# The first steps of a fused attention and two-layer-network kernel, issued from a written list of named steps

## The chip, the cores and the metric

The kernel runs on one core of one Trainium2 chip. The metric is the device time of one execution in microseconds (us), and the number compared is the median of several executions. The engines are named as the profile names them: PE is TensorE (matmuls; PEld its weight loads), DVE is VectorE, ACT is ScalarE, POOL is GpSimd, and SP is the engine whose queue issues nearly all DMAs. Each engine runs its own instructions strictly in the order in which the program issued them. What an instruction needs from another engine it waits for, and everything behind it on its engine waits too.

## What is computed

Attention over pooled keys and values (8 batches, 8 heads, 576 rows, pooling by 8 to 72 keys), then two networks on the 4608 resulting rows of 512 numbers. This change touches only the beginning: the attention of the first rows and `h = x @ w_in` with the first steps behind it.

```python
k_p = k.reshape(B, H, Sp, pool, D).mean(axis=3)      # pool = 8, Sp = 72
v_p = v.reshape(B, H, Sp, pool, D).mean(axis=3)
scores = scale * np.matmul(q, k_p.transpose(0, 1, 3, 2))
scores = scores - np.max(scores, axis=-1, keepdims=True)
attn = np.exp(scores)
attn = attn / (np.sum(attn, axis=-1, keepdims=True) + 1e-09)
x = np.matmul(attn, v_p)            # then rows x 512
h = x @ w_in                        # 4608 x 512 @ 512 x 2048
g = h * np.cos(h)
y = g @ w_out                       # 2048 x 512; a second network follows
```

## The kernel before

**Tiling.** The 4608 rows are nine blocks of 512. A block's attention runs over four pairs of heads. Its result x is kept as a high and a low part, four pairs of them, one for each quarter of the 512 columns. The first matrix product is cut in units: a unit is one block times 256 columns of `w_in`, that is two chunks of 128 columns, and has eight slots of three matmuls each (line 652: high by high, high by low, low by high). Slots 0 to 3 of a unit use its first chunk with x quarters 0 to 3, slots 4 to 7 its second chunk. Counted over the whole kernel, slot 64 is the first slot of unit 8. The first sixteen units take blocks 0 and 1 in turn (`units_h`): units 0 to 4 are block 0 with chunks 0 to 9, units 5 to 9 block 1 with the same chunks, units 10 to 15 the other six chunks for both blocks.

**A chunk of weights** comes as 64-bit words and is turned into a high and a low float part by class `Chunk`: `load` (an SP DMA), `s1` (two ACT instructions, lines 114 and 115), `bits` (three DVE instructions, 119, 123 and 127), `join` (POOL, 139), then the high part by ACT (line 1173) and the low part by POOL (line 1174).

**The attention of a block**, for each pair: scores on PE (line 449 for block 0, 414 for block 1), maximum and subtraction on DVE (460 to 470, 422 and 423), exponentials on ACT (464, 480), sums on DVE and a scaling of the exponentials (`norm`, lines 499 to 514) on POOL or DVE, transposes on PE (550, 528), a high part by ACT and a low part by DVE for each, the product with the values on PE (577), and x in two parts by ACT (579) and DVE (580). The keys of block 1 are pooled by PE (line 250), the values of both by PE (304, 307) and prepared on DVE, ACT and POOL (`prep_vn`).

**Behind a unit** runs `chain`: step 0 on ACT (663), step 1 on DVE (666), step 2 on ACT (669, a sine) and step 3 on DVE (671), which frees the unit's PSUM tile. There are three such tiles, so a unit cannot start before step 3 of the unit three before it. `g_store` sends the result to DRAM.

**What sets the order.** Block 0's attention is written out as plain calls, with the chunks advanced by `pipe.step()` (class `Pipe`) in between; a step runs the word operations of one chunk, the high and low part of the one before, and the first step of the next. Then a loop goes over the units' slots. Behind each slot's matmuls it issues the chain steps at fixed slots, a `pipe.step()` at slot 1 and in the first units at slot 5, and what `Attn.plan` has put in the list `work` for that slot. Block 1's plan is spread over the first five units by the factor `Q0 / NQ` = 5/8, block 2's begins at slot 64. So issue order is fixed by the program, and each engine sees its own share of it.

Of the kernel before, what the change touches and what calls it, by code (L numbers as in the profile page):

```python
# [20 lines left out]
POOL = 8  # L21
TWO_PI = 2.0 * math.pi
# [13 lines left out]
def fused_kernel(ctx, tc, qT_d, kT_d, vN_d, vM_d, vL_d, w_in, w_out, w2_in, w2_out, g_ln, out):  # L36
# [64 lines left out]
    class Chunk:  # L101
# [39 lines left out]
        def s2(self):  # L141
            self.bits()
            self.join()

        def s3(self):
            self.done(self)

# [22 lines left out]
    class Pipe:  # L170


        def __init__(self, chunks):
            self.todo = list(chunks)
            self.loaded, self.one, self.two = [], [], []

        def fill(self, most=8):

            held = [c.raw for c in self.loaded + self.one]
            while self.todo and len(held) < most:  # L180
                c, raw = self.todo[0]
                if raw is not None and any(raw is r for r in held):
                    break
                self.todo.pop(0)
                c.load(raw)
                held.append(raw)
                self.loaded.append(c)

        def step(self):
            last = self.two.pop(0) if self.two else None  # L190
            if self.one:
                c = self.one.pop(0)
                c.s2()
                self.two.append(c)
            if last:
                last.s3()
            self.fill()
            if self.loaded:
                c = self.loaded.pop(0)
                c.s1()  # L200
                self.one.append(c)

        @property
        def busy(self):
            return self.loaded or self.one or self.two or self.todo


# [13 lines left out]
    def kv_jobs(b, hf):  # L221


        def raw_tile(n):
            if b < 2:
                return wi.tile([P, n], F32, "kvraw")
            return wo.tile([P, n], F32, "kvraw")
# [6 lines left out]
        def k_job(i):  # L234
            p = 2 * hf + i
            raw = raw_tile(POOL * SP)
# [27 lines left out]
        def v_job(i):  # L264
# [3 lines left out]
            raw = raw_tile(POOL * D)  # L268
# [13 lines left out]
    def load_vn(b):  # L282
        if b == 0:
            t = [wi.tile([P, 2, BLK], F32, "vn") for _ in range(3)]
# [95 lines left out]
    class Attn:  # L380
# [49 lines left out]
        def scores0(self, p):  # L430
            self.e[p] = self.tile([P, TPB, 2, SP], F32, "e")
            e, qT = self.e[p], self.qT[p]
            if p != 2:
                pool, tag = (ps_q, "q") if p == 3 else (ps_y, "y")
                sc = pool.tile([P, 2, BLK], F32, tag=tag, name="sc")
                parts = [(sc[:, :, 0:4 * SP].rearrange("p u (t m) -> p u t m", t=2), 0, TPB)]
            else:
                parts = [(None, 2 * u, 2) for u in range(TPB // 2)]
            direct = p % 2 == 0
            if direct:  # L440
                self.sm[p] = ap2.tile([P, 2 * TPB], F32, tag="sm", name="sm", bufs=4)
            for sc, t0, nt in parts:
                if sc is None:
                    sc = ps_a.tile([P, 2, 2 * SP], F32, tag="a", name="sc")
                    sc = sc.rearrange("p (u t) m -> p u t m", u=1)
# [7 lines left out]
                u = nt // 2  # L453
                mx = ap2.tile([P, 2 * TPB], F32, tag="mx0", name="mx")[:, 0:2 * nt]
                mxv = mx.rearrange("p (u g) -> p u g", u=u)
                sc = sc.rearrange("p u t (a s) -> p u (t a) s", a=2)
                ev = e[:, t0:t0 + nt].rearrange("p (u t) a s -> p u (t a) s", u=u)
                if direct:
                    sm = self.sm[p][:, 2 * t0:2 * (t0 + nt)]
                    nc.vector.tensor_reduce(out=mxv, in_=sc, axis=AX.X, op=ALU.max, negate=True)  # L460
                    nc.vector.tensor_scalar(
                        out=mx, in0=mx, scalar1=SCALE, scalar2=None, op0=ALU.mult)
                    for g in range(2 * nt):
                        nc.scalar.activation(
# [713 lines left out]
    def now(fns):  # L1178
        for fn in fns:
            fn()  # L1180
# [355 lines left out]
```

## Time and profile before

| | us |
|---|---|
| median of 3 runs | 1328.03 (1328.01 to 1330.66) |
| the profiled execution, its own time | 1331.27 |
| its span, first to last instruction | 1329.5 |
| PE busy in the span | 1302.5 |
| DVE busy | 1053.0 |
| ACT busy | 697.9 |
| POOL busy | 504.5 |

The page shows busy time of each engine and the span in 40 slices of 33 us, with the clock that was granted to TensorE. A view of stretches gives the busy time between chosen instants. The view of waits says which engine stood still and what ended the wait. The timeline lists instructions in order of time, with equal ones merged. A wait is put down to the instruction that ended last before it.

### The profile page before, as it was taken

To read this page: it belongs to the slowest core of one execution; us is meant where nothing else is said; L and a number is where in the kernel's file an instruction comes from. 1 tells how busy PE (TensorE), PEld (TensorE's weight loads), DVE (VectorE), ACT (ScalarE), POOL (GpSimd) and SP (SyncE) were. 2 spreads that over 40 slices of the span, in tenths; PEclk is the share of its full clock that TensorE was granted. 3 is DMA by queue.
4 is the path that set the end of the run, shared out by engine and by line. 5 is a ranking of instruction groups with operands and counts; after the bars stand their busy time and mean duration, and the time that the engine had idled before them with its cause. 6 is when DMAs were issued, how large, how long until landed. Compare 5 with 4: busy or idle time off the path is not lost. (4 is left out here: it accounts for less than half of the span.)

```text
span 1329.5 us, 20583 instructions
## 1 busy us (share of the span) xinstructions
PE 1302.5 (98%) x7574; PEld 1140.3 (86%) x7574; DVE 1053.0 (79%) x1675; ACT 697.9 (52%) x987; POOL 504.5 (38%) x668
## 2 busy tenths in 40 slices
PE   6889999999999999999999999999999999999998
PEld 5768888888888888899999999998778888888887
DVE  7798888989788775879989889985687777776754
ACT  4576757756566657544444444443444444444432
POOL 3487678776574425301101001102434434343410
PEclk9899999999999999999999999999999999999999
DMA  8415567785674627655555455568310111111101
GB/s 287 172 68 191 187 231 270 254 289 188 222 254 145 226 98 255 234 196 158 172 141 176 132 173 175 160 219 341 105 56 33 56 40 49 47 45 51 40 25 40
DMA packets 82133, 206.09 MB, mean 155 GB/s; under 512 B 7920, under 2 KB 26352, under 8 KB 82032
## 3 DMA queue, kind: packets, MB, share of 16 engines
q1 hardware_dynamic: 81888, 204.77, 45.7%
q8 instruction: 60, 0.98, 0.3%
q14 instruction: 41, 0.34, 0.1%
q10 hardware_dynamic: 144, 0.00, 0.0%
HBM read 125.57 MB, written 79.17 MB: 154 GB/s over the span
## 5 line engine op out<-in xcount | busy, mean ns | idle before, releaser
L652 PE MATMUL h<-x,w 128*128 128x512 f32 x1728 | 433.6, 400 | 0.0
L652 PEld LDWEIGHTS h<-x,w 128*128 128x128 f32 x1728 | 316.5, 189 | 62.7 <-issue 2.2
L744 PE MATMUL y<-g,wy 128*128 128x256 f32 x3024 | 363.8, 283 | 1.3 <-DVE g L718 0.7
L744 PEld LDWEIGHTS y<-g,wy 128*128 128x128 f32 x3024 | 363.2, 192 | 1.9 <-DVE g L718 1.1
L716 ACT CAST g<-gs 128x1024 fp32r<-128x1024 f32 x72 | 75.7, 1051 | 173.2 <-PE y L744 86.1
L139 POOL TENSOR_TENSOR dec<-dec,raw 128x512 int32<-128x512 int32 x24 | 33.6, 1401 | 241.4 <-DVE dec L127 227.4
L718 DVE TENSOR_TENSOR g<-gs,g 128x1024 fp32r<-128x1024 f32 x72 | 90.5, 1257 | 34.2 <-ACT g L716 32.2
L669 ACT ACTIVATE t<-t,cst 128x1024 f32<-128x1024 f32 x72 | 83.1, 1154 | 62.3 <-DVE t L666 62.1
L974 POOL TENSOR_TENSOR yl<-yr,yh 128x1024 fp32r<-128x1024 f32 x18 | 43.9, 2439 | 153.7 <-ACT yh L969 117.6
L663 ACT ACTIVATE t<-h 128x1024 int32<-128x1024 f32 x72 | 73.5, 1020 | 53.7 <-PE h L652 53.5
L671 DVE TENSOR_TENSOR t<-t,h 128x1024 f32<-128x1024 f32 x72 | 87.3, 1212 | 11.9 <-ACT t L669 11.9
L666 DVE SCALAR_TENSOR_TENSOR t<-t,h 128x1024 f32<-128x1024 int32 x72 | 87.2, 1212 | 1.5 <-ACT t L663 1.5
L231 POOL TENSOR_TENSOR kvraw<-kvraw 128x256 f32<-128x256 f32 (+1 forms) x124 | 83.0, 670 | 11.5 <-DMA kvraw<-in_vM 3.5
L1105 POOL TENSOR_TENSOR sc<-sc,cst 128x1 f32<-128x1 f32 x36 | 20.3, 565 | 141.3 <-DVE sc L1094 114.0
L1140 ACT COPY o<-o 128x512 f32<-128x512 f32 x36 | 21.1, 587 | 96.4 <-PE o L1158 96.4
L698 DVE TENSOR_TENSOR gs<-gr,gs 128x256 f32<-128x256 f32 x136 | 65.9, 484 | 4.7
L718 DVE TENSOR_TENSOR g<-gr,g 128x768 fp32r<-128x768 f32 x68 | 69.1, 1017 | 0.0
L1156 PE MATMUL o<-w,lh 128*128 128x512 f32 x176 | 69.1, 393 | 0.0
L1158 PE MATMUL o<-w,ll 128*128 128x512 f32 x176 | 68.6, 390 | 0.0
L1157 PE MATMUL o<-w,lh 128*128 128x512 f32 x176 | 68.6, 390 | 0.0
L716 ACT CAST g<-gr 128x768 fp32r<-128x768 f32 x68 | 56.6, 833 | 0.0
L139 POOL TENSOR_TENSOR wf<-dec,raw 128x512 int32<-128x512 int32 x24 | 31.9, 1331 | 64.4 <-ACT eL L532 46.4
(191 smaller groups left out, 2572.3 us busy)
## 6 DMA issues: line engine op xcount, KB each, us to landing
gd<-t SPq DMA_DIRECT2D x72, 512.0 KB, 3.1
gr<-gd SPq DMA_DIRECT2D x68, 512.0 KB, 4.0
raw<-in_w_in SPq DMA_DIRECT2D x24, 512.0 KB, 4.4
raw<-in_w_out SPq DMA_DIRECT2D x24, 512.0 KB, 4.4
kvraw<-in_kT SPq DMA_DIRECT2D x32, 288.0 KB, 4.5
qT<-in_qT SPq DMA_DIRECT2D x36, 256.0 KB, 4.8
yd<-yo SPq DMA_DIRECT2D x36, 256.0 KB, 4.4
yr<-yd SPq DMA_DIRECT2D x18, 512.0 KB, 4.0
```

What stands on the lines that cost most here:

```text
L231: nc.gpsimd.tensor_tensor(out=x[:, 0:m], in0=x[:, 0:m], in1=x[:, m:2 * m], op=ALU.add)
L652: nc.tensor.matmul(h_ps[n][:, i], lhsT=w[:, a, kk, :], rhs=x[:, b], start=(kk == 0 and m == 0), stop=(kk == KD - 1 and m == 2),)
L663: nc.scalar.activation(out=t.bitcast(I32), in_=h, func=AF.Copy, scale=1.0 / TWO_PI, bias=0.25)
L666: nc.vector.scalar_tensor_tensor(out=t, in0=t.bitcast(I32), scalar=-TWO_PI, in1=h, op0=ALU.mult, op1=ALU.add)
L669: nc.scalar.activation(out=t, in_=t, func=AF.Sin, bias=halfpi)
L671: nc.vector.tensor_tensor(out=t, in0=t, in1=h, op=ALU.mult)
L716: nc.scalar.copy(out=o, in_=f)
L718: nc.vector.tensor_tensor(out=o, in0=f, in1=flat(g[i - 1])[:, 0:n * NH].bitcast(F32), op=ALU.subtract)
L744: nc.tensor.matmul(y_ps[j][i][:, NH * c:NH * (c + 1)], lhsT=w[:, a, P * c:P * (c + 1)], rhs=g[y][b], start=(q == 0 and c == 0 and k == 0), ...
L1156: nc.tensor.matmul(ps, lhsT=hi, rhs=w[:, 0], start=(c == 0), stop=False)
L1157: nc.tensor.matmul(ps, lhsT=hi, rhs=w[:, 1], start=False, stop=False)
L1158: nc.tensor.matmul(ps, lhsT=lo, rhs=w[:, 0], start=False, stop=(c == NF2 - 1))
```

## The change

The calls of the beginning, `Pipe`, and the plan of block 1 are gone. In their place each piece of work is a named step in a table, and a string `ORDER` lists 390 steps. Those ahead of the first `|` are issued before the first unit. Each following group, between two `|`, is issued behind the matmuls of one slot, for the first sixteen units (128 slots). From unit 16 on the old rule holds. Blocks 2 and on keep their plan.

The names: `LK`, `LQ`, `LV` are loads of keys, queries, values; a digit pair is block and pair. `S` scores (a: PE, b: DVE, c: ACT exponentials), `X` the exponentials of block 1, `N` norm (a: sums; b on POOL, `B` on DVE), `T`, `E` transposes (a PE, b ACT, c DVE), `V`, `P` values, `A` the x of a pair (a PE, b ACT, c DVE). `C5l`, `C5a`, `C5b`, `C5j`, `C5h` are load, `s1`, `bits`, `join` and high part of chunk 5; `C5o` is its low part on POOL, `C5O` on DVE. `H5.1` is chain step 1 of unit 5, `G5` its store.

The steps do what they did, but for two things. The low parts of chunks 0, 1, 2, 3, 5, 9, 10, 13 and 15 are on DVE (all sixteen were on POOL). Of block 0's four scalings pair 0's is on DVE and pairs 1 to 3 are on POOL (pairs 1 and 3 were on DVE, 0 and 2 on POOL). The scores of block 0's pair 2 are two steps for its two halves. The order of the first loads changes as well, and `mx0` has four buffers in place of two. Which SBUF slot a block 0 or 1 tile takes follows from the order of issue.

```diff
+ORDER = """
+LK00 LQ00 LK01 LG LK02 LQ01 LQ02 LK03 C0l LQ03 LV0 LK11 C2l LV1 LK13 C4l C3l LQ11 C1l LK12 LK10
...
+C1j C1h A02b C2b K10 C1O C2j A03c K11 C3a S100a C3b C3j C2h C2O C6l K12 C4a | A02c |  |  |  |
...
-        def s2(self):
-            self.bits()
-            self.join()
...
-    class Pipe:
-        def step(self):
-            last = self.two.pop(0) if self.two else None
-            if self.one:
-                c = self.one.pop(0)
-                c.s2()
-                self.two.append(c)
-            if last:
-                last.s3()
-            self.fill()
-            if self.loaded:
-                c = self.loaded.pop(0)
-                c.s1()
-                self.one.append(c)
...
-            def scale():
-                for i, (p, e) in enumerate(zip(ps, es)):
-                    i2 = p % 2
-                    eng = nc.vector if self.j == 0 and i2 else nc.gpsimd
+            def scale(i, eng):
+                p, e = ps[i], es[i]
+                i2 = p % 2
...
-            nc.gpsimd.tensor_tensor(
-                out=t[:, 1], in0=c.f, in1=t[:, 0].bitcast(F32), op=ALU.subtract)
...
+        def lo(eng):
+            eng.tensor_tensor(
+                out=t[0][:, 1], in0=c.f, in1=t[0][:, 0].bitcast(F32), op=ALU.subtract)
...
+        steps.update({f"C{f}l": load, f"C{f}a": c.s1, f"C{f}b": c.bits, f"C{f}j": c.join,
+                      f"C{f}h": hi, f"C{f}o": lambda: lo(nc.gpsimd), f"C{f}O": lambda: lo(nc.vector)})
...
+        places = [line.split() for line in ORDER.strip().split("|")]
+        for name in places[0]:
+            steps[name]()
...
                 h_mm(n, s // KD, s % KD)
-                if n > 1 and s == 3:
-                    chain(n - 2, 3)
-                if n > 0 and s in (0, 4, 7):
-                    chain(n - 1, (0, 4, 7).index(s))
-                if n > 1 and s == 5:
-                    g_store(n - 2)
-                if s == 1 and pipe.busy or s == 5 and n < Q0 - 1:
-                    pipe.step()
+                if n < 2 * NQ:
+                    for name in places[1 + SL * n + s]:
+                        steps[name]()
+                else:
...
                 for fn in work[SL * n + s]:
                     fn()
```

How this moves instructions shows in the order in which each engine gets them. `raw_170` to `raw_173` are the word buffers of chunks 0 to 3, `raw` that of a later chunk; `kT_90` to `kT_93` are the key tables of batch 0, `kT_94` to `kT_97` those of batch 1.

DVE, block 0's first pairs, before: the sums of pair 0 stand behind the maximum and subtraction of pair 1, and the scaling of pair 0 is not here (POOL has it).

```order
L460 TENSOR_REDUCE mx<-sc 128x8
L461 TENSOR_SCALAR mx<-mx 128x8
L243 TENSOR_REDUCE kp<-kvraw 128x72
L245 COPY kT_92<-kp 64x72
L246 COPY kT_92<-kp 64x72
L469 TENSOR_REDUCE mx<-sc 128x8
L470 TENSOR_TENSOR e<-sc,mx 128x576
L502 TENSOR_SCALAR sm<-sm 128x8
L503 RECIPROCAL sm<-sm 128x8
```

The same place on DVE now.

```order
L439 TENSOR_REDUCE mx<-sc 128x8
L441 TENSOR_SCALAR mx<-mx 128x8
L220 TENSOR_REDUCE kp<-kvraw 128x72
L222 COPY kT_92<-kp 64x72
L223 COPY kT_92<-kp 64x72
L485 TENSOR_SCALAR sm<-sm 128x8
L486 RECIPROCAL sm<-sm 128x8
L491 TENSOR_TENSOR em<-e,sm 128x4x128
L496 TENSOR_TENSOR el<-e,sm 128x4x32 x2
L439 TENSOR_REDUCE mx<-sc 128x8
L444 TENSOR_TENSOR e<-sc,mx 128x576
```

The scaling of pair 0 has come to DVE, and pair 1's maximum and subtraction stand behind it.

DVE, the end of block 0's attention (line 580) and the first scores of block 1 (422, 423), before.

```order
L580 TENSOR_TENSOR x<-xo,x 128x512 x2
L119 TENSOR_SCALAR dec<-dec 128x512
L123 TENSOR_SCALAR dec<-dec 128x512
L127 SCALAR_TENSOR_TENSOR dec<-raw_172,dec 128x512
L119 TENSOR_SCALAR dec<-dec 128x512
L123 TENSOR_SCALAR dec<-dec 128x512
L127 SCALAR_TENSOR_TENSOR dec<-raw_173,dec 128x512
L119 TENSOR_SCALAR dec<-dec 128x512
L123 TENSOR_SCALAR dec<-dec 128x512
L127 SCALAR_TENSOR_TENSOR dec<-raw,dec 128x512
L422 TENSOR_REDUCE mx<-sc 128x4
L423 TENSOR_TENSOR e<-sc,mx 128x288
```

The same place now; line 1151 is a low part on DVE.

```order
L564 TENSOR_TENSOR x<-xo,x 128x512
L141 TENSOR_SCALAR dec<-dec 128x512
L145 TENSOR_SCALAR dec<-dec 128x512
L149 SCALAR_TENSOR_TENSOR dec<-raw_173,dec 128x512
L1151 TENSOR_TENSOR w<-dec,w 128x512
L564 TENSOR_TENSOR x<-xo,x 128x512
L141 TENSOR_SCALAR dec<-dec 128x512
L145 TENSOR_SCALAR dec<-dec 128x512
L149 SCALAR_TENSOR_TENSOR dec<-raw,dec 128x512
L399 TENSOR_REDUCE mx<-sc 128x4
L400 TENSOR_TENSOR e<-sc,mx 128x288
L1151 TENSOR_TENSOR w<-dec,w 128x512
```

The words of chunks 0 to 3 are now done before the last x of block 0, and one chunk's words, not three, stand between that x and the first scores of block 1.

PE, the first units, before.

```order
L652 MATMUL h<-x,w 128x512 x6
L414 MATMUL sc<-kT_90,qT 64x144
L414 MATMUL sc<-kT_94,qT 64x144
L414 MATMUL sc<-kT_94,qT 128x144
L652 MATMUL h<-x,w 128x512 x3
L250 MATMUL kp<-kvraw,ident 128x72 x8
L652 MATMUL h<-x,w 128x512 x3
L414 MATMUL sc<-kT_94,qT 128x144 x2
L652 MATMUL h<-x,w 128x512 x6
```

The same place on PE now.

```order
L227 MATMUL kp<-kvraw,ident 128x72 x16
L391 MATMUL sc<-kT_90,qT 64x144
L391 MATMUL sc<-kT_94,qT 64x144
L391 MATMUL sc<-kT_94,qT 128x144
L227 MATMUL kp<-kvraw,ident 128x72 x8
L628 MATMUL h<-x,w 128x512 x15
L391 MATMUL sc<-kT_94,qT 128x144 x2
L628 MATMUL h<-x,w 128x512 x3
L227 MATMUL kp<-kvraw,ident 128x72 x8
```

Three of the four key poolings and the first half of block 1's first scores now stand ahead of the first unit, and five slots of that unit run before the second half of the scores.

## Rows read from the trace of the kernel before

**Rows 1.** The page's 40 slices of the span: PE busy in tenths.

```profile
PE   6889999999999999999999999999999999999998
```

**Rows 2.** Stretches of the span: busy us (and instructions) of each engine, clock.

```profile
core 0: us, PE busy (x) PEld busy (x) DVE busy (x) ACT busy (x) POOL busy (x), PEclk, DMA share, GB/s
0.00:38.77 38.77, 26.51 (x122) 21.59 (x122) 28.91 (x72) 18.97 (x59) 15.65 (x36) 0.91 0.81 276
...
0.00:101.81 101.81, 81.54 (x389) 64.89 (x390) 83.94 (x154) 60.30 (x127) 59.26 (x83) 0.92 0.51 177
60.00:101.81 41.81, 37.90 (x189) 28.98 (x188) 40.39 (x64) 32.47 (x50) 33.02 (x39) 1.00 0.19 69
101.81:119.50 17.69, 17.69 (x79) 14.65 (x78) 16.24 (x16) 11.19 (x15) 13.88 (x15) 1.00 0.45 154
119.50:200.00 80.50, 80.50 (x410) 67.09 (x409) 66.38 (x101) 52.82 (x68) 55.65 (x83) 1.00 0.60 214
28.00:34.00 6.00, 5.06 (x15) 3.75 (x15) 5.67 (x12) 3.04 (x7) 2.19 (x2) 0.50 0.31 93
48.00:58.00 10.00, 9.21 (x34) 8.05 (x35) 4.95 (x9) 3.26 (x8) 5.21 (x4) 0.51 0.43 151
```

**Rows 3.** Waits of PE, 0 to 100 us: total, times, longest.

```profile
PE sc L449 <- DVE kT L246: 5.2, 1, 5.2
PE sc L414 <- DVE e L423: 4.1, 1, 4.1
PE eTp L550 <- DVE eT L555: 3.0, 2, 1.7
```

**Rows 4.** Timeline of PE: start, us, what; in brackets the idle before.

```profile
49.72 2.94 PE L652 MATMUL h<-x,w 128*128 128x512 f32 x6
...
99.77 19.90 PE L652 MATMUL h<-x,w 128*128 128x512 f32 x87
119.50 0.65 PE L414 MATMUL sc<-kT,qT 128*128 128x144 f32 x4
```

**Rows 5.** Waits of DVE, 0 to 102 us.

```profile
DVE mx L422 <- PE sc L414: 5.6, 2, 4.9
...
DVE eL L533 <- ACT eL L532: 2.2, 1, 2.2
```

**Rows 6.** Timeline of DVE and ACT up to 11 us.

```profile
0.84 0.65 DVE L1221 MEMSET kT<- 128x144 f32 x4 [0.84 <-PEq L1522]
...
7.55 0.76 DVE L460 TENSOR_REDUCE mx<-sc 128x8 f32<-128x576 f32 x1 [2.38 <-PE sc L449]
...
10.78 0.76 DVE L469 TENSOR_REDUCE mx<-sc 128x8 f32<-128x576 f32 x1 [0.61 <-PE sc L449]
10.90 0.24 ACT L464 ACTIVATION_READ_ACCUMULATOR e<-sc,mx 128x1 f32 x1
```

**Rows 7.** Timeline of all engines, 43 to 48 us: word steps beside POOL's work.

```profile
43.63 0.69 DVE L127 SCALAR_TENSOR_TENSOR dec<-raw,dec 128x512 int32<-128x512 int32 x1
...
44.24 0.42 DVE L119 TENSOR_SCALAR dec<-dec 128x512 f32<-128x512 f32 x1
44.56 1.28 POOL L139 TENSOR_TENSOR dec<-dec,raw 128x512 int32<-128x512 int32 x1 [1.24 <-DVE dec L127]
44.70 1.42 DVE L123 TENSOR_SCALAR dec<-dec 128x512 int32<-128x512 int32 x1
45.79 1.44 POOL L1174 TENSOR_TENSOR w<-dec,w 128x512 fp32r<-128x512 f32 x1
...
46.15 1.63 DVE L127 SCALAR_TENSOR_TENSOR dec<-raw,dec 128x512 int32<-128x512 int32 x1
```

**Rows 8.** Timeline of DVE: a scaling of block 0, and block 1's last x.

```profile
18.01 0.69 DVE L509 TENSOR_TENSOR em<-e,sm 128x512 f32<-128x512 f32 x1
18.62 0.49 DVE L514 TENSOR_TENSOR el<-e,sm 128x128 f32<-128x128 f32 x2
...
101.13 0.68 DVE L580 TENSOR_TENSOR x<-xo,x 128x512 fp32r<-128x512 f32 x1
```

More of the change, by code (lines that the diff above doesn't have):

```diff
@@ L283, in load_vn @@
         if b == 0:
-            t = [wi.tile([P, 2, BLK], F32, "vn") for _ in range(3)]
+            t = [wi.tile([P, 2, BLK], F32, "vn", i) for i in range(4, 7)]
         else:
@@ L435, in scores0, with mm @@
                 sc = pool.tile([P, 2, BLK], F32, tag=tag, name="sc")
[L436 to L438 removed]
+                sc = sc[:, :, 0:4 * SP].rearrange("p u (t m) -> p u t m", t=2)
+                t0, nt = 0, TPB
+            else:
+                sc = ps_a.tile([P, 2, 2 * SP], F32, tag="a", name="sc")
+                sc = sc.rearrange("p (u t) m -> p u t m", u=1)
+                t0, nt = 2 * u0, 2
             direct = p % 2 == 0
[L440 removed]
+            if direct and u0 == 0:
                 self.sm[p] = ap2.tile([P, 2 * TPB], F32, tag="sm", name="sm", bufs=4)
[L442 to L445, printed above, removed]
+            u = nt // 2
+            mx = ap2.tile([P, 2 * TPB], F32, tag="mx0", name="mx", bufs=4)[:, 0:2 * nt]
+            mxv = mx.rearrange("p (u g) -> p u g", u=u)
+            sv = sc.rearrange("p u t (a s) -> p u (t a) s", a=2)
+            ev = e[:, t0:t0 + nt].rearrange("p (u t) a s -> p u (t a) s", u=u)
+            def mm():
                 for i in range(nt):
@@ L474, in scores0, with exps @@
                     )
-            if not direct:
-                self.exp(p)
+            def exps():
+                if not direct:
+                    return self.exp(p)
+                sm = self.sm[p][:, 2 * t0:2 * (t0 + nt)]
+                for g in range(2 * nt):
+                    nc.scalar.activation(
+                        out=ev[:, g // 4, g % 4], in_=sv[:, g // 4, g % 4], func=AF.Exp,
+                        bias=mx[:, g:g + 1], scale=SCALE, accum_out=sm[:, g:g + 1],
+                    )
+            return mm, less, exps
         def exp(self, p):
@@ L581, in av @@
                     out=x[:, 1], in0=o, in1=x[:, 0].bitcast(F32), op=ALU.subtract))
-        def now(self, name, *a):
-            for fn in getattr(self, name)(*a):
-                fn()
         def plan(self, put):
@@ L637, in fused_kernel @@
     gd = [dram.tile([P, NQ, 2, BLK], F32, tag="gd", name=f"gd{j}") for j in range(NB)]
-    w_in_t, w_op = [], [{} for _ in range(NQ)]
+    w_in_t, w_op = {}, [{} for _ in range(NQ)]
+    steps = {}
     h_ps, h_t, g_raw, g_sum, g_t, y_ps = {}, {}, {}, {}, {}, {}
@@ L1270, in fused_kernel @@
-        now(prep_vn(0, 1))
-        a0.now("av", 1)
-        a0.now("e_tr", 3)
-        a0.now("e_tr_left", 1)
-        pipe.step()
-        a0.now("av", 2)
-        add(1, 0, "k0")
-        a0.now("av", 3)
-        add(1, 0, "k1")
-        pipe.step()
-        early = {7: raws[1], 9: raws[2], 11: raws[3]}
-        pipe.todo += [(order[i], early.get(i)) for i in range(6, len(order))]
-        pipe.step()
+            in_=m_key.rearrange("p (o s) -> p o s", o=1)[:, :, 0:KL].to_broadcast([P, 16, KL]))
```

279 lines of the change are left out of this document (137 added, 142 removed).

## The prediction

> **What bounds the kernel now.** I read the slices first [rows 1]. PE is at 9 tenths or more everywhere but in the first two slices, so only the beginning has anything to give. The stretches then put numbers on it [rows 2]: up to 101.81 us PE is busy for 81.54, so it idles 20.27 us, and behind that it has no gap (17.69 of 17.69 us, then 80.50 of 80.50). Part of the busy time is slow as well: in 28 to 34 and 48 to 58 us the granted clock is half (0.50, 0.51, the 1.2 GHz level) while PE is busy 5.06 and 9.21 us, which at full clock would be some 7.1 us less. The waits say whom PE waits for [rows 3]: DVE, nearly always. So next I look at DVE: up to 101.81 us it is busy 83.94 us and idle 17.87, and in 60 to 101.81 us only 1.42 of 41.81 is idle [rows 2]. Its own waits are for PE (5.6 us) and ACT (2.2 us) [rows 5]. The picture is a ring: early on DVE idles because PE has not been fed, and later PE idles because DVE is behind.
>
> The measuring point is the first score matmul of block 2, behind slot 64, at 119.50 us [rows 4]. Both orders have the same PE work ahead of it and, but for two chunks' words and a few low parts, the same work behind it. Since PE has no gap behind it, what is won up to that point stays won unless a new gap opens.
>
> **The change part by part.**
>
> *DVE's work up to block 1's last x.* Before, that x ends at 101.81 us [rows 8], when DVE has done the words of 13 chunks, four chain steps 1 and three chain steps 3. In the new order the same counts stand ahead of it. Added are six low parts (chunks 0, 1, 2, 3, 5, 9). Removed is one scaling, since block 0 had two on DVE and keeps one: 0.69 + 0.49 = 1.18 us [rows 8]. The trace shows no low part on DVE. The nearest row is line 127, which has the same 128x512 shape and two SBUF inputs: 0.69 us with POOL still, 1.63 us while POOL runs its own low part [rows 7]. I take 0.69, because the same change takes six low parts of about 1.44 us [rows 7] off POOL in this stretch, so six 0.69 = 4.1 us; the upper end is 9.8, and a cost of nothing is excluded since the instructions are real. DVE's work becomes 83.94 + 4.1 - 1.2 = 86.9 us.
>
> The rows show that a word step which starts beside a POOL instruction takes 1.42 us, where its like takes 0.42, and ends 0.3 us after that one (46.12 against 45.84) [rows 7]. The Trainium skill, "SBUF — State Buffer", section "SBUF: two separate sides", says that a VectorE instruction with two SBUF inputs, or in a two-port mode, and a GpSimd instruction hold one port pair exclusively, for a whole instruction. That speaks against low parts on DVE: by it each could wait out a POOL instruction, and the six would cost up to 6 x (0.69 + 1.44) = 12.8 us. The trace agrees that the two hinder each other, but its dearest row is 1.63, not 2.13.
>
> *DVE's idle time.* Before it is 17.87 us, 9.86 of it before 38.77 us [rows 2]. What must stay: the start (0.84 us); of the wait for the first scores (2.38) I keep 0.9, since most of the mask work now stands behind the first key table and fills it; and 1.0 us until ACT has delivered pair 0's last sum at 11.14 us, for which DVE now waits before anything of pair 1 [rows 6]. That is 2.7 us where 3.8 were (0.84 + 2.38 + 0.61). Behind it DVE idled 9.86 - 3.8 = 6.0 us up to 38.77. I went through DVE's new order there and asked at each step whether its input is ready. It mostly is: as I reckon it, pair 2's exponentials end on ACT at 18.5 us and their sums come up on DVE at 19. The waits for a high part on ACT (2.2 us [rows 5]) have other work in them. I leave half, 3.0 us. So DVE should finish block 0's last x near 28.9 busy before, plus two more chunks' words (3.1, two of 0.42 + 0.42 + 0.69), plus three low parts (2.1), less a scaling (1.2), plus 5.7 idle = 38.6 us, with four chunks' words done, not two. From there I take the rate of 60 to 101.81 us, 1.42 / 41.81, for 55 us: 1.9. Together 2.7 + 3.0 + 1.9 = 7.6 us. The bounds are 2.7 and 17.87.
>
> *The point that follows.* Block 1's last x then ends at 86.9 + 7.6 = 94.5 us. In the issue list it is A12c behind slot 41, and slot 42 is the first to read it. From there to the point are 22 slots of three matmuls; 87 of them took 19.90 us [rows 4], so 66 take 15.1. The point is at 94.5 + 0.1 + 15.1 = 109.7 us, 9.8 earlier.
>
> *Is PE itself there by 94.5 us?* PE's work to slot 42 is the busy time up to 99.77 us, 79.5, plus seven slots more (4.8), less 7.1 for the half clock: 77.2 us. Idle remain 5.2 us at the start [rows 3] and, by the same walk through the order, some 4.4 in short waits of block 0's transposes, together 86.8. One stretch at half clock, as before, adds 2.5 to 4.6 us and still ends at 91.4 at most. So DVE is last, by 3 us or more. A check on the way: the fifth slot, at 49.72 us before [rows 4], needs all four x of block 0 and chunk 1, which come near 38.6; PE should run it by 42, so 8 of the 9.8 us should already be won there.
>
> *POOL, ACT, loads.* POOL loses six low parts and gains a scaling, and was busy 59.26 of 101.81 us [rows 2]; its cover is DVE, which is later throughout. ACT has the same instructions and as many table loads. The first loads are the same bytes; the first two keys and the first query stay in front. On SP, chunk 9's load now stands behind the first key load of batch 2, whose SBUF slot is free by then, and the loads of chunks 14 and 15 behind the second, which waits for POOL's scaling of block 1's last pairs; both are wanted only behind slot 64. The first store of g stands behind those key loads; chain step 0 of unit 3 needs it, and some 6 us of DVE work lie between. All this at nothing; if a load came late, what it costs is a chunk's delay, in the range below.
>
> *What is given back.* Behind the point DVE still has the words of chunks 14 and 15 and the low part of 15, which used to be done. In the next 80.50 us DVE idles 14.1 [rows 2]. Two chunks at 1.5 to 3.5 us each (the low end as above, the high end 0.42 + 1.42 + 1.63 [rows 7]) fit, but they stand ahead of the chain step 3 of unit 6 that unit 9 needs. With ample cover it costs nothing, with none 3.7 to 8.6 us; the first is much nearer, so 1.0 us.
>
> **Sum.** 9.8 - 1.0 = 8.8 us. The profiled execution took 1331.27 us, of which 1.77 lie around its span of 1329.5; it becomes 1322.5. It was 3.24 us slower than the median of 1328.03, which becomes **1319.2 us**.
>
> **The rivals.**
>
> *The port price.* DVE's low parts run beside POOL's instructions, since the new order packs both engines closer, and each costs 1.63 us: 5.6 us more. The last x is at 100.1, the point at 115.3, and with the give-back the median is 1324.8. For it: POOL is busy 33.02 of 41.81 us in 60 to 101.81 [rows 2]. Against it: what leaves POOL also leaves off stretching DVE's word steps. The Trainium skill's rule above would make it 3.0 us worse still, 1327.8.
>
> *The clock.* PE waits in short pieces for block 0's transposes at 20 to 30 us, and the half clock came right after such a place, at 28 us [rows 2]. If PE runs 10 to 20 us at half clock between 26 and 60, its 86.8 becomes 92 to 97 us, by 97 it and not DVE is last, and the median is 1319 to 1322.
>
> *Slower.* The gaps stay. Each low part on DVE ends a chain of DVE words, POOL join, ACT high part. Issued too early, it holds DVE until these are done, and with it the scores and x behind it. If DVE idles as long as before (17.87 us) and the low parts come on top, the last x is at 104.8 us, or 110.4 at 1.63 each; the point is at 120.0 to 125.6 and the median, with the give-back, 1329.5 to 1335. It decides from 16.4 us of idle time on. Against it: in the new order such a low part has a chunk's words ahead of it, which cover the chain.
>
> *Nothing.* The gaps return by half or more through steps whose lateness I did not see (gaps of 14 to 17 us): 1325.4 to 1328.7. That the order would not reach the chip is excluded: the engines' lists differ.
>
> **How the numbers follow.** Forecast (1313 to 1323) 0.57, port price 0.12, clock 0.09, nothing 0.09, slower 0.11, better than 1313 0.02. A measurement of this kernel can tell about 0.2%, 2.7 us, from no change, so faster ends at 1325.4 and slower begins at 1330.7. A third of the port case lies above 1325.4, and a fifth of the slower case, with cheap low parts, under 1330.7. That gives faster 0.76, same 0.15, slower 0.09. The range runs from 1313, where idle time is near its lower bound of 2.7 us (4.9 less than I take, and a little off the stretched word steps), to 1327; it leaves out the slower case, half of nothing, and the tails.
>
> **What would show it.** Right: DVE idles under 10 us up to the last x; that x ends near 94 us; the first unit's fifth slot begins near 42; PE's idle time to the point is near 11 us and the long half-clock stretch at 48 to 58 is gone; low parts on DVE take about 0.7 us. Wrong: low parts above 1.2 us (port price); DVE waits for ACT's high parts adding to over 8 us (slower); granted clock 0.5 for over 10 us (clock); PE waits for chain steps 3 behind unit 8 (give-back).

## The result

The changed kernel takes **1317.07 us** (median of 5 runs, 1315.31 to 1317.49) where the kernel before took 1328.45 in the same session (5 runs, 1328.01 to 1331.32). The ratio is 0.9905, with a 95% interval of 0.9891 to 0.9920: 11.4 us faster by the medians. 1319.2 was predicted, 1313 to 1327 as the range. The profiled execution took 1317.37 us with a span of 1315.5; it is close to its median, whereas that of before (1331.27) lay 2.8 us over its own, so the two traces differ by 13.9 us.

The page's slices: before, the first three lay below 9 (6, 8, 8) [rows 1], one more than the prediction read. In the changed kernel the second is at 9; the first (6) and the third (8) are as they were.

```profile
PE   6989999999999999999999999999999999999998
```

Stretches of the changed kernel (us from start to end of the stretch, its length, then busy us and instructions of each engine, granted clock, DMA). Block 0's last x ends at 38.68 us, block 1's at 88.86, the measuring point (first score matmul of block 2) is at 105.71.

```profile
core 0: us, PE busy (x) PEld busy (x) DVE busy (x) ACT busy (x) POOL busy (x), PEclk, DMA share, GB/s
0.00:38.68 38.68, 28.00 (x153) 21.74 (x153) 33.38 (x78) 22.95 (x69) 20.25 (x40) 1.00 0.80 286
0.00:88.86 88.86, 74.60 (x393) 58.48 (x394) 78.57 (x156) 59.13 (x126) 54.65 (x82) 1.00 0.59 211
0.00:105.71 105.71, 91.45 (x468) 72.42 (x469) 90.78 (x172) 68.29 (x138) 60.96 (x89) 1.00 0.59 210
105.71:200.00 94.29, 94.29 (x482) 78.60 (x481) 82.07 (x124) 64.67 (x86) 69.01 (x98) 1.00 0.57 201
48.00:58.00 10.00, 10.00 (x50) 7.70 (x49) 9.34 (x21) 6.34 (x11) 5.95 (x8) 1.00 0.13 51
```

The point moved from 119.50 [rows 4] to 105.71, 13.8 us; from there to the end of the span it takes 1209.8 us where it took 1210.0. So everything was won ahead of the point and nothing given back. The same stretch of before, up to its point:

```profile
0.00:119.50 119.50, 99.23 (x467) 79.54 (x468) 100.18 (x169) 71.49 (x141) 73.14 (x97) 0.93 0.50 174
```

Up to the point PE is busy 91.45 us where it was busy 99.23, at a granted clock of 1.00 where it was 0.93. So of the 13.8 us, 7.8 are shorter busy time at a higher clock, for nearly the same matmuls (468 and 467 on record), and 6.0 are idle time (14.26 against 20.27).

PE's timeline (start, us, what; in brackets the idle before it and what ended it):

```profile
36.88 3.97 PE L628 MATMUL h<-x,w 128*128 128x512 f32 x15
40.69 0.65 PE L391 MATMUL sc<-kT,qT 128*128 128x144 f32 x4
...
82.66 0.52 PE L561 MATMUL xo<-eT,vM 128*128 128x64 f32 x3 [1.81 <-DVE eT L539]
...
86.65 19.22 PE L628 MATMUL h<-x,w 128*128 128x512 f32 x84
105.71 0.65 PE L391 MATMUL sc<-kT,qT 128*128 128x144 f32 x4
```

The first row is the first five slots, so the fifth runs near 40 us, where it ran at 49.72 [rows 4]: 9.7 of the 13.8 us are won there. The last 84 matmuls are slots 36 to 63, so slot 42 begins near 86.65 + 6 x 0.69 = 90.8 us.

DVE's words of weights, grouped by line, up to block 1's last x (count | busy us, mean ns | idle before). Line 149 answers to 127 of before, 141 to 119, 145 to 123; line 1151 is the low part. Ahead of it the three lines of before, same grouping, up to 102 us:

```profile
L119 DVE TENSOR_SCALAR dec<-dec 128x512 f32<-128x512 f32 x14 | 10.8, 774 | 0.6 <-ACT dec L114 0.6
L127 DVE SCALAR_TENSOR_TENSOR dec<-raw,dec 128x512 int32<-128x512 int32 x13 | 10.8, 829 | 0.4
L123 DVE TENSOR_SCALAR dec<-dec 128x512 int32<-128x512 int32 x13 | 10.1, 776 | 0.4
```

```profile
L149 DVE SCALAR_TENSOR_TENSOR dec<-raw,dec 128x512 int32<-128x512 int32 x13 | 9.4, 720 | 0.4
L141 DVE TENSOR_SCALAR dec<-dec 128x512 f32<-128x512 f32 x13 | 7.5, 577 | 0.3 <-ACT dec L136 0.3
L145 DVE TENSOR_SCALAR dec<-dec 128x512 int32<-128x512 int32 x13 | 7.0, 540 | 0.4
...
L1151 DVE TENSOR_TENSOR w<-dec,w 128x512 fp32r<-128x512 f32 x6 | 4.6, 763 | 0.0
```

A chunk's words took 0.774 + 0.776 + 0.829 = 2.38 us of DVE before and take 1.84 now: 7.1 us less over 13 chunks, more than the six low parts (4.6 us) cost.

### The profile page after: what moved, and what is told of

Its sections match the earlier page's. It is cut to its first block, busy times and chain, and to the rows that moved or that the text cites. A ratio compares the mean times of both kernels' runs of the same rounds, so it can differ in the third digit from the quotient of the medians.

```text
span 1315.5 us, 20565 instructions
## 1 busy us (share of the span) xinstructions
PE 1294.9 (98%) x7574; PEld 1132.8 (86%) x7574; DVE 1045.4 (79%) x1681; ACT 695.0 (53%) x985; POOL 497.0 (38%) x662
```

## The experiments

The runs ask four things: which half of the change gives the gain, what a wait of PE costs through the clock, what the late loads cost, and what block 0's scalings do. Ratios are to the kernel before, run in the same session; the median of before was between 1328.45 and 1330.34 in the four sessions, so ratios are the fairer comparison between kernels of different sessions. The point is that of the one profiled run, whose own time is in the last column: in e2, e7 and before (point 119.50, 1331.27 us) it lies 2.8 to 3.8 us over the median. The "new order" is the changed kernel.

| kernel | edit | median us | ratio (95%) | point us | profiled run, us |
|---|---|---|---|---|---|
| changed | | 1317.07 | 0.9905 (0.9891 to 0.9920) | 105.71 | 1317.37 |
| e1 | new order, all low parts on POOL | 1323.23 | 0.9949 (0.9935 to 0.9962) | 111.49 | 1322.86 |
| e2 | old order, the nine low parts on DVE | 1328.42 | 0.9992 (0.9982 to 1.0002) | 120.28 | 1331.92 |
| e7 | new order, low parts 0 to 3 on DVE | 1318.93 | 0.9916 (0.9899 to 0.9932) | 110.67 | 1322.76 |
| e8 | new order, low parts 5, 9, 10, 13, 15 on DVE | 1320.85 | 0.9927 (0.9913 to 0.9941) | 106.58 | 1321.08 |
| e3 | old order, one pipe step behind the scores | 1329.89 | 1.0002 (0.9989 to 1.0014) | 117.49 | 1328.77 |
| e6 | new order, a wait forced on PE | 1322.55 | 0.9942 (0.9925 to 0.9959) | 111.98 | 1323.84 |
| e10 | e6, the wait filled with matmuls | 1319.45 | 0.9929 (0.9916 to 0.9941) | 107.44 | 1318.88 |
| e11 | old order, its wait filled with matmuls | 1328.08 | 0.9990 (0.9978 to 1.0003) | 115.08 | 1327.89 |
| e4 | new order, chunk 15's first step later | 1315.76 | 0.9898 (0.9883 to 0.9913) | 103.89 | 1315.29 |
| e5 | new order, loads of chunks 14, 15 earlier | 1315.34 | 0.9896 (0.9883 to 0.9910) | 103.59 | 1315.27 |
| e9 | new order, block 0's old scalings | 1318.43 | 0.9917 (0.9900 to 0.9933) | 105.92 | 1317.35 |
| e12 | e4 with block 0's old scalings | 1317.95 | 0.9916 (0.9902 to 0.9930) | 108.33 | 1319.55 |

### The two parts of the change, one at a time

**e1**, the new order without the low parts on DVE (chunks 9, 10, 13 and 15 likewise).

```diff
-... C0h C0O ... C1O ... C2O ... C3O ... C5O ...
+... C0h C0o ... C1o ... C2o ... C3o ... C5o ...
```

> The new order with all nine low parts put back on POOL, at the same places of the list. Theory 1 (the order closes the gaps of PE and DVE, the low parts hardly matter): DVE has six times 0.76 us less to do before the last x of block 1, the word steps stretch a little again, and the median stays at 1317 to 1320 us. Theory 2 (the gain comes from taking work off POOL, so that DVE's word steps no longer wait beside it): the word steps go back from 1.84 to some 2.4 us a chunk, DVE's last x ends 5 us or more later than 88.9, and the median is 1323 us or more. A third possibility: POOL's own queue becomes late, since a low part there holds the joins behind it; then ACT and DVE wait for joins and high parts, and the median is 1321 to 1326.

**e2**, the old order with the same nine low parts on DVE.

```diff
-            nc.gpsimd.tensor_tensor(
+            (nc.vector if f in (0, 1, 2, 3, 5, 9, 10, 13, 15) else nc.gpsimd).tensor_tensor(
```

> The kernel before, in its old order, with the low parts of chunks 0, 1, 2, 3, 5, 9, 10, 13 and 15 on DVE. Theory 1 (the order): nothing is won; DVE, which is last from 60 to 102 us, gets 4 to 5 us more work and less stretching, so 1326 to 1331 us, and the wait of 4.1 us with the half clock behind it is still there. Theory 2 (the port): word steps fall to under 2 us a chunk, DVE's last x comes 3 to 5 us earlier, 1322 to 1325.

The order alone gives about half of the gain (ratio 0.9949), the low parts alone give nothing that can be measured (0.9992), both together 0.9905. So the parts are not additive. Of the two theories each failed in one run: the order alone does not bring 1317 to 1320 us, and fewer stretched words alone, in e2, do not bring 1322 to 1325. Where the gain of the low parts comes from shows in e1. A chunk's words take 0.688 + 0.785 + 0.787 = 2.26 us there (up to 102 us), against 1.84 in the changed kernel. Up to block 1's last x (94.55 us in e1) DVE is busy 81.86 us without the six low parts, and 78.57 with them in the changed kernel. In e1, DVE's timeline beside POOL's low parts (chunk 4's words and the first scores of block 1):

```profile
39.06 1.26 DVE L141 TENSOR_SCALAR dec<-dec 128x512 f32<-128x512 f32 x1
40.36 1.41 DVE L145 TENSOR_SCALAR dec<-dec 128x512 int32<-128x512 int32 x1
41.80 1.66 DVE L149 SCALAR_TENSOR_TENSOR dec<-raw,dec 128x512 int32<-128x512 int32 x1
43.38 0.45 DVE L399 TENSOR_REDUCE mx<-sc 128x4 f32<-128x288 f32 x1
```

In the changed kernel the three took 0.94, 0.43 and 0.69 us, and the scores were read 2.7 us earlier:

```profile
40.65 0.45 DVE L399 TENSOR_REDUCE mx<-sc 128x4 f32<-128x288 f32 x1
```

In e1 PE waits for them:

```profile
44.37 3.31 PE L227 MATMUL kp<-kvraw,ident 128*128 128x72 f32 x16 [1.87 <-DVE e L400]
```

The 16 matmuls in this row take 3.31 us, in the changed kernel 1.90: behind the wait PE is at half clock (0.50 in 46 to 50 us). The same later scores, in e1 and in the changed kernel:

```profile
52.24 0.91 PE L391 MATMUL sc<-kT,qT 128*64 128x144 f32 x6
```

```profile
46.55 0.91 PE L391 MATMUL sc<-kT,qT 128*64 128x144 f32 x6
```

Here 5.7 of the 5.8 us by which e1's point is later have arisen: 2.5 by the end of the wait (44.37 against 41.87 us), and 3.2 in the 32 matmuls behind it, which take 7.9 us, not 4.7. So a low part left on POOL costs stretched words, and where the scores wait for these words, a wait of PE and, more than that in this run, the clock. The third possibility named above, late joins on POOL, does not show as the cause: ACT's waits for joins sum to 9.2 us up to 110 us in e1 and to 8.5 in the changed kernel.

In e2 the words are relieved as well (0.784 + 0.455 + 0.706 = 1.95 us for a chunk's, 5.6 us less over 13 chunks), but the seven low parts up to 102 us take 953 ns each. DVE also waits for high parts there, as a view of its waits from 60 to 122 us shows (total, times, longest):

```profile
DVE w L1174 <- ACT w L1173: 4.8, 3, 3.6
```

The low parts' 6.7 us use up the 5.6 us, and PE still stands 3.08 us at block 1's first scores; the profile puts this wait down to a key copy on ACT. The longest of DVE's waits, 3.6 us, stands at 121 us, behind the point. It is the wait that the rival "slower" spoke of, too late to matter for the point. In the changed kernel DVE's only such wait up to the point is one of 2.2 us behind block 1's last x.

Within the order, the changed order of the first loads, the four buffers of `mx0` and the two halves of pair 2's scores were not tried by themselves; what each gives is open.

**e7** and **e8** ask which low parts matter: e7 puts back those of chunks 5, 9, 10, 13 and 15, e8 those of 0 to 3.

> The new order with the low parts of chunks 0 to 3 alone on DVE; those of 5, 9, 10, 13 and 15 are back on POOL. All nine back on POOL cost 6 us. Theory that this loss came from the first four: on POOL they stretched DVE's words at 39 to 43 us, the first scores of block 1 came 1.8 us later, PE waited and lost its clock; then this kernel loses next to nothing, 1316.5 to 1319, with the point near 106. Theory that every low part on POOL costs its share (six of them lie ahead of the point, two of these on POOL here): 1319 to 1320.5.

> The complement: the low parts of chunks 0 to 3 on POOL, those of 5, 9, 10, 13 and 15 on DVE, in the new order. Theory that the first four make the loss: as with all nine on POOL, 1321.5 to 1324, a PE wait of 1 to 3 us at 44 us and half clock behind it. Theory of equal shares: 1320 to 1321.5, with no such place needed.

e8 shows the predicted wait of PE (1.91 us), but not the half clock behind it; its ratio lies 0.0022 over the changed kernel's, that of e7 0.0011, and all the intervals touch. The median of e7 fits the first theory, that of e8 the second. So this does not tell the two theories apart. The profile of e7, taken of the slowest of its six runs, shows what a later low part can cost: POOL does the scaling of block 1's last pairs later, and PE waits 1.30 us for it. The key load that needs POOL's scaling is late as well (73.94 us, not 71.68) and with it chunk 15's load behind it (see "The loads that I put at nothing"): ACT waits 4.20 us for that load, and PE 2.23 us for a transposed part on DVE.

```profile
75.94 0.63 PE L512 MATMUL eLp<-ident,el 128*128 128x128 f32 x4 [1.30 <-POOL el L496]
...
84.50 0.85 PE L561 MATMUL xo<-eT,vM 128*128 128x64 f32 x3 [2.23 <-DVE eT L539]
...
85.37 1.47 PE L561 MATMUL xo<-eT,vM 128*128 128x448 f32 x3
```

The last of these rows took 0.85 us in the changed kernel, so this wait too was followed by the half clock (0.50 from 84.50 to 88.50 us).

### The clock

**e3** moves unit 0's pipe step from slot 1 behind slot 3's work in the old order, so that DVE reads the first scores of block 1 ahead of another chunk's words.

```diff
-                if s == 1 and pipe.busy or s == 5 and n < Q0 - 1:
+                if n and s == 1 and pipe.busy or s == 5 and n < Q0 - 1:
...
+                if n == 0 and s == 3:
+                    pipe.step()
```

> The kernel before with one pipe step of the first unit moved from slot 1 to slot 3, so that on DVE the words of chunk 4 stand behind the first subtraction of block 1's scores and not ahead of it. Theory (the wait of 4.1 us of PE for that subtraction costs twice, once itself and once through the half clock that follows): the wait falls to about 1 us, no long stretch at half clock follows, and the median is 1320 to 1324 us. Rival (the half clock has another cause, or DVE's later work is what counts, so that the time saved here is waited out behind 60 us): the median is 1326 to 1329 us.

The wait of 4.1 us [rows 3] shrank to 0.64, and one of 3.53 us came up 7 us later, with the half clock behind it (this row's six matmuls take 0.91 us at full clock):

```profile
45.37 0.73 PE L414 MATMUL sc<-kT,qT 128*128 128x144 f32 x4 [0.64 <-DVE e L423]
...
52.74 1.53 PE L414 MATMUL sc<-kT,qT 128*64 128x144 f32 x6 [3.53 <-issue]
```

The profile names no releaser for the longer wait. The last to end before it were ACT's key copy (52.72 us) and DVE's subtraction of the next scores (52.65), which here stood behind the words of the step that was moved. Nothing was won: 1329.89 us where the theory had 1320 to 1324. This wait could not be taken out alone.

**e6** forces such a wait on the new order, **e10** fills it.

```diff
-C4b S100b S101a C3h C3O C5l C5a C5b C4j C4h
+C4b C3h C3O C5l C5a C5b S100b S101a C4j C4h
```

> The new order with one edit: DVE's maximum and subtraction on the first scores of block 1 (40.65 and 41.13 us, lines 399 and 400) stand behind the low part of chunk 3 (1.21 us there) and the words of chunk 5 (three instructions, 1.53 us), so they end at some 45 us and not 41.6. The key pooling on PE at 41.87 us needs the PSUM tile they read, so PE should stand still for about 3 us there. In the old order a wait of 4 us at this place was followed by 10 us at half clock, in the new order there is neither. Theory that the wait brings the half clock: a granted clock near 0.5 for 6 to 10 us behind the wait, and PE, which was last at the end of block 1's attention, arrives 3 us later for the wait and 3 to 4 us for the clock, less what its later short waits take up (1.8 us at most): the point at 110 to 112.5 us, the median at 1321.5 to 1324. Theory that the half clock has another cause: clock 1.00 throughout, only the wait is paid, the median at 1318 to 1320.5.

```diff
                 h_mm(n, s // KD, s % KD)
+                if n == 0 and s == 5:
+                    for r in (0, 1, 0, 1):
+                        h_mm(n, 1, r, True)
```

> The new order with the forced wait of the kernel of the last call (maximum and subtraction of block 1's first scores behind the low part of chunk 3 and the words of chunk 5), and twelve more matmuls on PE (four slots of unit 0 once more into the open sum, 2.7 us) where it stood still for 2.84 us. So PE is as late by work as it was by waiting. These matmuls change h of unit 0. Theory that standing still brings the half clock, which took 3.3 us more for the same 29 matmuls there: the granted clock stays at 1.00, the point moves from 111.5 us, where the forced wait alone puts it, to about 108, the median is 3 to 3.5 us under it, ratio 0.9915 to 0.9925. Theory that the half clock belongs to this place or to the work behind it, not to the wait: half clock at 46 to 52 us again, ratio 0.994.

PE in e6, and the stretch of 46 to 54 us there (columns as above):

```profile
45.54 3.54 PE L227 MATMUL kp<-kvraw,ident 128*128 128x72 f32 x16 [2.84 <-DVE e L400]
48.82 1.63 PE L628 MATMUL h<-x,w 128*128 128x512 f32 x3
50.38 2.40 PE L391 MATMUL sc<-kT,qT 128*64 128x144 f32 x10
```

```profile
46.00:54.00 8.00, 8.00 (x36) 6.28 (x36) 2.32 (x6) 1.60 (x4) 1.36 (x2) 0.59 0.52 207
```

The same place in e10, and the same stretch:

```profile
41.23 3.71 PE L628 MATMUL h<-x,w 128*128 128x512 f32 x15
45.04 2.00 PE L227 MATMUL kp<-kvraw,ident 128*128 128x72 f32 x16
46.84 0.94 PE L628 MATMUL h<-x,w 128*128 128x512 f32 x3
47.72 1.40 PE L391 MATMUL sc<-kT,qT 128*64 128x144 f32 x10
```

```profile
46.00:54.00 8.00, 8.00 (x50) 6.26 (x50) 5.13 (x12) 5.27 (x10) 0.87 (x1) 1.00 0.48 190
```

PE is held up about as long in both (the key pooling starts at 45.54 and 45.04 us), by waiting in the one and by work in the other. Only the one that waited fell to half clock. Those 29 matmuls took 7.6 us against 4.3, the point came 4.5 us later. The other runs agree: the mean granted clock was 0.999 to 1.000 in the five runs of e10, within 1318.88 to 1321.74 us, and 0.994 to 0.999 in the ten of e6, within 1319.53 to 1329.36. That standing still here brings the half clock is shown, and the theory's numbers for e6 (point at 110 to 112.5, median 1321.5 to 1324) held. What it costs is less sure: 3.1 us by the two medians, 1.7 by the ratios, whose intervals overlap. e10's ratio of 0.9929 is a little over the 0.9915 to 0.9925 expected. The Trainium skill, "TensorE: Matmul & The Clock Gate", section "HAM oscillation — how this bites in real kernels", says the same of a kernel whose PE waits for data between its pieces of work; this case agrees.

**e11** fills the wait of the old order, ahead of the fourth slot.

```diff
+                if n == 0 and s == 3:
+                    for r in (0, 1, 2, 0, 1, 2):
+                        h_mm(n, 0, r, True)
                 h_mm(n, s // KD, s % KD)
```

> The old order with eighteen more matmuls (six slots of unit 0 once more, 4.1 us) ahead of the fourth slot, where PE stood still from 44.7 to 48.8 us for block 1's scores. These matmuls change h of unit 0. Theory that standing still brings the half clock: clock 1.00 at 48 to 58 us, PE reaches 58 us some 4.5 us earlier, DVE gets block 1's scores earlier by as much (it idled 4.9 us for them), and the point moves from 119.5 to 115.5 to 117, the ratio is 0.997 to 0.998. If the clock returns but DVE is last anyway by its own work: clock 1.00 and ratio 0.999 to 1.0005. If the half clock has another cause: 0.50 as before, ratio 1.000.

The clock did come back, and the point moved to 115.08:

```profile
48.00:58.00 10.00, 9.87 (x60) 7.80 (x59) 8.44 (x15) 5.69 (x13) 5.38 (x5) 1.00 0.64 226
```

Yet the ratio is 0.9990, and its interval holds both of the numbers expected for a clock that returns. Part of the difference is that 119.50 comes from a run 2.8 us over its median, and that e11 takes 1211.0 us from the point on, not 1210.0. The clock came back in the other runs too: the mean granted clock is 0.997 at the median of e11's eleven runs, against 0.995 for before in that session. What the half clock at 48 to 58 us costs a typical run of the old order stays open between nothing and 2.9 us. So the half clock behind this wait does not explain the gain. The earlier stretch of half clock [rows 2] is still there in e11 (0.50 in 26 to 34 us), as in e2 and e3; no run took it away by itself.

### The loads that I put at nothing

In the changed kernel the wait of 1.81 us at 82.66 came from a chain. ACT stood for chunk 15's words, with block 1's transposes queued behind them, and DVE stood for ACT. ACT, then DVE:

```profile
79.65 0.69 ACT L136 ACTIVATE dec<-raw 128x512 f32<-128x512 f32 x1 [2.84 <-DMA raw<-in_w_in]
80.23 0.66 ACT L137 ACTIVATE raw<-raw 128x512 int32<-128x512 uint32 x1
80.79 0.61 ACT L1148 ACTIVATE w<-dec 128x512 fp32r<-128x512 f32 x1
81.31 1.06 ACT L538 CAST eT<-eTp 128x512 fp32r<-128x512 f32 x2
```

```profile
81.91 1.29 DVE L539 TENSOR_TENSOR eT<-eTp,eT 128x512 fp32r<-128x512 f32 x2 [2.84 <-ACT eT L538]
```

And SP's queue, which issued nothing from 42.65 to 71.68 us. It stood at a key load, by the profile 25.3 us for sums on DVE and 3.7 us for a scaling on POOL. Only then came the two chunks:

```profile
42.21 0.44 SPq L131 DMA_DIRECT2D raw<-in_w_in  x1
71.68 0.33 SPq L214 DMA_DIRECT2D kvraw<-in_kT  x1
72.11 0.85 SPq L131 DMA_DIRECT2D raw<-in_w_in  x2
```

**e4** moves the step, **e5** the loads.

```diff
-... | E11a E11b |  | C15a C11b ...  | T12b T12c G1 T13a T13b | ...
+... | E11a E11b |  | C11b ...  | T12b T12c G1 T13a T13b C15a | ...
```

> The new order with one name moved: the first ACT step of chunk 15 goes from slot 29 to slot 33, behind the high parts of the last transposes of block 1. Theory (this step waits 2.8 us on ACT for its load, which stands on SP behind a key load, and behind it ACT, DVE and PE wait): PE's wait of 1.8 us for the transposes' low parts goes and the span is 1.5 to 2 us shorter, 1315 to 1316 us. Rival (PE is then held by the last x on DVE or by the words of later chunks): under 0.7 us, 1316.5 to 1317.5.

```diff
-... C13l P10c P11a P11b | ... C10j H2.1 | C14l P11c ... | A11c C15l C11a ...
+... C13l C14l C15l P10c P11a P11b | ... C10j H2.1 | P11c ... | A11c C11a ...
```

> The new order with the loads of chunks 14 and 15 issued on SP's queue right behind that of chunk 13, ahead of block 2's keys and the stores of g; chunk 15's first step on ACT stays where it was. Theory that this load was late because it was queued: ACT's wait of 2.84 us at 79.65 goes, and with it the waits of DVE and of PE (1.81 us at 82.66); the point at 104 to 104.5 us, the ratio as with the step moved, 0.989 to 0.990. Rival: two more loads in the stretch where chunk 13 comes hold other transfers up, or the word buffers come free too late and block the queue: ratio 0.9905 or more.

Both take the wait away, and the point comes 1.8 and 2.1 us earlier, as e4's and e5's theory had it. In e5 ACT has the words in time:

```profile
76.21 0.57 ACT L516 CAST eL<-eLp 128x512 fp32r<-128x512 f32 x1
76.67 0.68 ACT L136 ACTIVATE dec<-raw 128x512 f32<-128x512 f32 x1
```

The load was late because it was queued; that is shown. That these two kernels are faster than the changed one rests on the profiles, since the intervals of the ratios overlap. They are the best versions found, at 0.9896 and 0.9898.

### The scalings

**e9** puts block 0's scalings back, pairs 0 and 2 on POOL, 1 and 3 on DVE; **e12** does the same on e4.

```diff
-N00B ... N01b ... N03b
+N00b ... N01B ... N03B
```

> The new order with block 0's scalings where they were: pairs 0 and 2 on POOL, pairs 1 and 3 on DVE. My reckoning: one scaling more on DVE, 0.69 + 0.49 = 1.2 us, in the stretch to block 0's last x at 38.68 us, where DVE is nearly always busy, so that x, the fifth slot and the point come 1 us later: 1317.5 to 1319. Rival: in the new order pair 0's scaling on DVE stands ahead of pair 1's maximum, and POOL's for pairs 1 and 3 keep PE waiting (0.57 and 0.84 us for the transposes at 18.24 and 24.61, 0.33 and 0.69 behind them), so with pairs 1 and 3 on DVE these waits go and nothing is lost, or up to 2 us is won: 1315 to 1317.

> The new order with chunk 15's first step moved later (no wait of 1.8 us at 82 us) and block 0's scalings where the old order had them. In the new order the old scalings made the fifth slot 1.7 us later (42.35 against 40.69 us for the scores behind it), yet the point was where it was, since the wait at 82.66 us took it up (0.38 of 1.81 us left). If that is so, here the 1.7 us stay: point at 105.3 to 106, median 1.5 us over that of the moved step alone, ratio 0.9905 to 0.9915. Rival, that the scalings cost nothing in themselves: the point stays near 104, ratio 0.9895 to 0.990.

In e9 the median of 1318.43 lies in my range, but not by my reckoning, since the point did not come 1 us later. The scores behind the fifth slot come at 42.35 us, not 40.69, but the point at 105.92, only 0.2 later: the wait at 82.84 us shrank from 1.81 to 0.38 us. Of the 1.7 us at the fifth slot, 1.5 are longer busy time of PE (31.48 us up to these scores, 30.01 in the changed kernel). Part of that is half clock, which came up again some 2.5 us behind a wait of 1.37 us at 26.91 us:

```profile
28.00:34.00 6.00, 5.42 (x22) 3.85 (x22) 5.90 (x12) 4.34 (x10) 2.88 (x6) 0.72 0.70 271
```

In e12 the wait at 82 us is gone, and the ratio goes from 0.9898 to 0.9916, as expected; but the intervals overlap, so a loss is not shown. The point is at 108.33 us where 105.3 to 106 was expected. PE waited 1.70 us for the table that POOL builds behind pair 0's scaling, and was slow behind it (3.78 us for eight matmuls). In e9 it waited as long there (1.78 us), and the eight took 2.00:

```profile
14.47 3.78 PE L281 MATMUL vps<-vn,pool_w 128*128 128x256 f32 x8 [1.70 <-POOL pool_w L1207]
```

## Why the prediction was right, and where its steps failed

**The place and the size held.** All is won ahead of the point, the fifth slot came near 40 where 42 was said, and the half-clock stretches are gone. But the sum itself was too small by 5.1 us: 8.8 us were expected of a profiled run that gave 13.9. The last step, from the profile to the median, hid 2.9 of it: the 3.24 us by which the profile of before lay over its median were taken to remain, and the new profile lies 0.30 over its own. That the forecast came within 2.1 us of the median is in this part luck.

**DVE to block 0's last x: right, to 0.1 us.** 38.6 was reckoned. It ended at 38.68, with 33.38 busy and 5.30 idle.

**DVE's work up to block 1's last x: over-sized by 8.3 us.** 86.9 was reckoned, 78.57 measured. The low parts cost 4.6 where 4.1 were taken. What the sum left at its old price are the words: they shrank by 7.1 us, most of it because POOL no longer runs the low parts beside them (e1: 0.42 us of 0.54 a chunk). The other 1.7 us are spread over further DVE instructions, among them line 316 (2.1 us where line 339 took 3.0). I named this effect only as a bound (1313) and as an argument against the port price, and did not put it in the sum. Rows 7 had its size: a step that starts beside POOL took 1.42 where its like takes 0.42.

**DVE's idle time: 10.3 us, not 7.6.** Up to block 0's last x it was 5.30 where 5.7 was reckoned; behind it 4.99, not 1.9, and 2.84 of that is one wait, the one for chunk 15 above. "All this at nothing; if a load came late, what it costs is a chunk's delay" is the step that failed. The load waited behind a key load that waited for DVE and then for POOL (the prediction had named POOL), and a chunk wanted only behind slot 64 held ACT, whose next instructions were wanted at once.

**"DVE is last, by 3 us or more": wrong.** DVE ended at 88.86, PE came to slot 42 only at 90.8: PE was last by 1.9 us. DVE was earlier than reckoned, and PE later. Its busy time up to there was as reckoned (76.5 against 77.2), but it idled 14.26 us, not 9.6: 10.68 up to 36.88 us, where I had 5.2 and some 4.4 for all, and 3.58 in 60 to 86.65, where I had none. PE's waits for the first scores came to 6.1 us, not 5.2, and 1.81 of the later 3.58 are the chain behind chunk 15's load again. The two errors work against each other: DVE's x came 5.6 us early, PE's extra idle time took back some 1.9 of that, and the point came 4.0 us early (105.71 against 109.7). The bound that I gave for PE's arrival (91.4) did hold. So two of the signs named for "right" did not come, DVE's idle time under 10 us (10.3) and PE's near 11 (14.3).

**The give-back: none**, 1.0 us was taken.

**The port price did not come.** Eight low parts on DVE up to 102 us took 0.74 us on the mean, one of them 1.21, where the rival had 1.63 each. By the rule of the Trainium skill, "SBUF — State Buffer", section "SBUF: two separate sides", that the prediction weighed, six would have taken up to 12.8 us; they took 4.6. The runs show the hindrance from the other side: with all low parts on POOL (e1) it is DVE's words that are stretched. In the old order (e2) the same low parts took 0.95 us and waited.

## What to carry to other kernels

When work is moved from one engine to another that shares something with it, put into the sum what the first engine's relief gives to everything that ran beside it; here that was more than the moved work cost. Issue a load, and the step that consumes it, apart from work that is urgent on the same in-order queues: a step that nobody needs yet can hold an engine whose next instruction is needed at once. A wait on TensorE is to be priced with the slow matmuls behind it, and removing one wait of a row of late steps may win nothing (e3, e11), so order and placement are best tried together.

## What the runs showed of the hardware

A wait on PE was followed by half clock (1.2 GHz) after 4.10 us (before), 3.53 (e3), 3.08 (e2), 2.84 (e6), 2.23 (e7) and 1.87 us (e1), but also after 1.71 us in e3 and 1.37 us in e9 (there some 2.5 us behind the wait):

```profile
23.40 0.63 PE L550 MATMUL eTp<-ident,em 128*128 128x128 f32 x4 [1.71 <-DVE eT L555]
```

It was not after 1.91 (e8), 1.81 (changed kernel), 1.70 (e2, at 89.14 us) or 1.37 us (e12). So the length of the one wait does not decide it; what else does was not tried. e6 and e10 price one such fall: 3.2 us for 29 matmuls.

The granted clock does not show all of it. At the start of every kernel, and in e12 until some 22 us, the rows give a clock of 1.00 while matmuls take nearly twice their later time, as the row of 3.78 us above. In the changed kernel, the first scores of block 0 and the last:

```profile
5.45 4.50 PE L433 MATMUL sc<-kT,qT 128*128 128x144 f32 x16 [5.45 <-DVE kT L223]
...
15.98 1.25 PE L433 MATMUL sc<-kT,qT 128*128 128x144 f32 x8
```

The Trainium skill, "TensorE: Matmul & The Clock Gate", section "Seeing it yourself", warns that the records of clock events have been seen to be unreliable on trn2. These two rows agree with that, 0.28 us a matmul and 0.16 at one recorded clock. Here durations were the surer sign.

Runs of the kernel before spread over 8 us (1327.37 to 1335.36 beside e1 to e4), and between these two the mean granted clock falls from 0.996 to 0.990, 0.006 x 1330 = 8 us. With the clock at 0.999 to 1.000, the runs of e4 stay within 2.6 us. The changed kernel, e4 and e5, with shorter waits on PE, were steadier as well as faster.
